# Clustered attention and a rotary token mixer on one core: seven products in batches three and four only, sums of weights made over two plain batches by way of DRAM, a fixed order of all engines from the third batch on

## The chip, the cores and the metric

The kernel runs on one core of one Trainium2 chip. The metric is the device time of one launch in microseconds (us); less is better. The core has five engines that take part: TensorE (PE, matrix products; PEld is its weight load), VectorE (DVE), ScalarE (ACT), GpSimd (POOL) and SyncE (SP), which here issues nearly all DMAs.

## The reference

There are 4 batches, 8 heads, 768 tokens and 64 columns a head, so 512 channels. Queries and keys see each other only if their nearest of 16 centroids is the same; the result x of that attention goes through a mixer of tokens and a product over channels:

```python
mask = q_assign[:, :, :, None] == k_assign[:, :, None, :]
scores = np.where(mask, scale * np.matmul(q, k.transpose(0, 1, 3, 2)), -1000000.0)
...
x = attn_out.transpose(0, 2, 1, 3).reshape(B, S, H * D)    # 4 x 768 x 512

theta = x @ w_theta                                        # 512 x 512
zr, zi = x * np.cos(theta), x * np.sin(theta)
yr = np.einsum('ts,bsd->btd', w_tok_r, zr)                 # 768 x 768
yi = np.einsum('ts,bsd->btd', w_tok_i, zi)
u = x + yr + yi
return u + np.maximum(u @ w_ch, 0.0)                       # 512 x 512
```

## The kernel before

**Two halves.** The attention (lines up to 840) is a loop over units of heads and token tiles and ends at about 450 us. It writes x, with channels on the partitions, into a DRAM buffer for each batch (xT_d). The mixer reads it back. Nothing of the attention is changed.

**The mixer of one batch** works on six tiles of 128 tokens. For each tile *theta* (L927) loads the columns (load_columns, tile xs) and, in another layout, the blocks (load_blocks, L640 to 650, four DMAs, tile xb), and then goes through: a hi part xh on ACT and a lo part xl on DVE (rotation_parts); twelve matmuls with w_theta on PE (rotation_angle, tile tp); reduction of the angle modulo two pi on DVE (rotation_reduce, L666 to 668, tiles kk and rab); abs on ACT (L670); the transpose of xb into xn on DVE (L652); and in *rotate* two sines on ACT (L950) and two products on DVE (L952). Rotations are written two tiles ahead of the mix that uses them (AHEAD = 2).

All matrix products are done with each fp32 operand cut into a hi and a lo part and three products, hi by hi, hi by lo and lo by hi. The hi part is a copy on ACT to PE's own 32-bit type, the lo part a subtraction on POOL or DVE.

**The first batch is mixed plainly** (L985): per tile 48 matmuls into the six PSUM banks of y. The weights wr and wi of all six tiles lie in SBUF as hi and lo. Then *channel_first* (L1138) adds y to x, splits the sum u (add_y), makes u @ w_ch in eight groups of twelve matmuls (channel_products, L1127) and writes out (channel_out, L1134, tile ot and its store L1136).

**Batches two to four use seven products.** Per token tile the two matrices wr and wi and the two halves of zr and zi make a 2 x 2 by 2 x 2 product, for which seven products of sums take the place of eight (ORDER, W_SUM, Z_AT, Y_AT). It works on 256 channels at a time, so each batch has two halves, h = 0 with tiles 0 to 5 and h = 1 with tiles 5 to 0; a half tile has 21 matmuls (mix_forms, L1079). The second half's z go through DRAM: zd is stored by rotate and read back as zb by *split_z* (L1042), which makes the sums of z on DVE (L1054, 1055, 1057) and splits them on ACT and POOL (L1063, 1064). *add_products* (L1083) adds the products to x in seven instructions on DVE (L1088).

**The sums of weights** ("forms", seven 384 KB tiles for each token tile) are made by *make_forms* (L1018) while the first batch runs: it loads wr and wi as fp32 (tile raw), makes a sum on DVE, a copy on ACT and a subtraction on POOL or DVE. The forms of tiles 1, 2 and 3 stay in SBUF in the place of plain weights that are done with. Those of tiles 4, 5 and 0 do not fit; they go to DRAM (w_f) and are loaded again in each batch (*load_forms*, L1038): tile 4's into the four buffers us that later hold u, tiles 5's and 0's into the same seven buffers one after the other (the spares ws0 to ws3 and the first of wr0 and wi0).

**What sets the order.** In the mixer before, each engine's order is decided by the scheduler of the tile framework, from the order in which the code is written and from what is ready by its own reckoning. In the attention, a function *in_order* chains each engine's instructions in the order of the code. SP takes its DMAs in its own row; one that waits holds all behind it.

Of the kernel before, what the change touches and what calls it, by code (L numbers as in the profile page):

```python
# [41 lines left out]
def kernel(  # L42
# [884 lines left out]
    def theta(b, t):  # L927
        n, name = b * NT + t, f"{b}_{t}"
        load_columns(n + 1)
        xs = columns.pop(n) if b else xts[b][:, :, t * P:(t + 1) * P]  # L930
        xh, xl, xn, kk, rab = rotation_tiles(n, name)

        late = n == AHEAD
        rotation_parts(xs, xh, xl, last_out[0] if late else None)
        tp = pm[0].tile([P, 512], F32, tag="bank", name=f"tp{name}") if b else mbank(f"tp{name}")
        with behind(last_rows[0] if late else last_mix[0] if n == AHEAD + 1 else None):
            rotation_angle(xh, xl, tp)
        rotation_reduce(n, tp, kk, rab)
        rotation_turn(n, xn)
        rotate(b, t, rab, xn)  # L940

    z_d = {}

    def rotate(b, t, rab, xn):
        if b == 0:
            z = mz.tile([P, 2, 2, DM], F32R, tag="z", name=f"z{b}_{t}")
        for x, (sc_, bi_) in enumerate(((-1.0, halfpi), (1.0, 0.0))):
            tr = rab[:, x]
            with tc.issue_after(before_sin[0].ins):
                sine = nc.scalar.activation(out=tr, in_=tr, func=AF.Sin, scale=sc_, bias=bi_)  # L950
            with tc.issue_after(before_mul[0].ins):
                nc.vector.tensor_tensor(out=tr, in0=tr, in1=xn, op=ALU.mult)  # L952
            if b == 0:
# [4 lines left out]
        if b:  # L958
            zs[b, t] = rab
            z_d[b, t] = dram.tile([P, 2, DM // 2], F32, tag=f"z{t}", name=f"zd{b}_{t}", bufs=2)  # L960
            nc.sync.dma_start(out=z_d[b, t], in_=rab[:, :, DM // 2:DM])
            return
# [22 lines left out]
    def mix(t):  # L985
        for d in range(NCT):
            for w, (zh, zl) in zip((w_r[t], w_i[t]), zs[0, t]):
# [22 lines left out]
    KEPT = (4, 5, 0)  # L1010
    w_f = {t: dram.tile([P, 7, S], F32, name=f"wf{t}") for t in KEPT}
    PLACE = {
        4: (24, 25, 26, 27, 0, 1, 2), 5: (3, 4, 5, 6, 7, 8, 9), 0: (24, 25, 26, 27, 0, 1, 2),
        1: (10, 11, 12, 13, 14, 15, 3), 2: (4, 5, 6, 7, 8, 9, 16), 3: (17, 18, 19, 20, 21, 22, 23)}
# [3 lines left out]
    def make_forms(t):  # L1018

        raw = u_tile(f"raw{t}").rearrange("p c s -> p (c s)").bitcast(F32)  # L1020
        for x, k in enumerate("ri"):
            nc.sync.dma_start(out=raw[:, x * S:(x + 1) * S], in_=w_d[t, k])
        part = raw.rearrange("p (x n) -> p x n", x=4)
        sums = u_tile(f"sums{t}").rearrange("p c s -> p (c s)").bitcast(F32).rearrange("p (x n) -> p x n", x=4)
        for x, m in enumerate(ORDER):
            to = subs[PLACE[t][x]]
            hi, lo = to[:, 0:HS], to[:, HS:S]
            p, op, q = W_SUM[m]
            src = part[:, p]
            if op is not None:  # L1030
                src = part[:, 1] if m == 6 else sums[:, {4: 0, 3: 1, 1: 2, 7: 3}[m]]
                nc.vector.tensor_tensor(out=src, in0=part[:, p], in1=part[:, q], op=op)
            nc.scalar.copy(out=hi, in_=src)
            (nc.vector if x in (1, 4) else nc.gpsimd).tensor_tensor(out=lo, in0=src, in1=f(hi), op=ALU.subtract)
            if t in KEPT:
                nc.sync.dma_start(out=w_f[t][:, m - 1], in_=f(to))

# [3 lines left out]

    def split_z(b, t, h):  # L1042

        if h == 0:
            src = zs.pop((b, t))
        else:
            src = mzb.tile([P, 2, HD], F32, tag="zb", name=f"zb{b}_{t}")
            nc.sync.dma_start(out=src, in_=z_d.pop((b, t)))
# [34 lines left out]
    def add_products(b, h):  # L1083
# [9 lines left out]
        add(x[:, 0:3:2], twice(4), ALU.add)  # L1093
        add(x[:, 1:4:2], twice(3), ALU.subtract)
        add(x[:, 0:4:3], twice(1), ALU.add)
        add(x[:, 0:4:3], y[:, 2:4, 0:HS], ALU.subtract)
        add(x[:, 1:3], y[:, 2:4, 0:HS], ALU.add)
        add(x[:, 0], product(7), ALU.subtract) if h else add(x[:, 3], product(6), ALU.add)
        add(x[:, 3], product(6), ALU.add) if h else add(x[:, 0], product(7), ALU.subtract)
# [38 lines left out]
    def channel_first():  # L1138
        us = [add_y(0, ch * HS, (ch + 1) * HS) for ch in range(2)]
        for x in range(2 * NCT):  # L1140
            ch, e = divmod(x, NCT)
            cp = (mbank(f"cp0_{x}") if x < 2 else y[:, x - 2])[:, 0:HS]
            channel_products(cp, e, us[ch], range(NCT))
            channel_out(0, e, ch, cp)

    def channel(b, us):
        for x in range(2 * NCT):
            ch, e = divmod(x, NCT)
            cp = product(ORDER[x % 7])
            for ds in ((0, 1), (2, 3)):  # L1150
                channel_products(cp, e, us[2 * ch:2 * ch + 2], ds)
            channel_out(b, e, ch, cp)
# [3 lines left out]
    late_weights = late()  # L1156
    made = {0: (4,), 2: (5, 0), 3: (1,), 4: (2,)}
    for t in range(NT):
        theta(*divmod(t + AHEAD, NT))
        weights_after[0] = splits[min(t + 1, len(splits) - 1)]  # L1160
        next(late_weights, None)
        mix(t)
        for x in made.get(t, ()):
            make_forms(x)
    channel_first()
    load_x(1)
    make_forms(3)
# [3 lines left out]
    four[0] = pm[1].tile([P, 512], F32, tag="bank", name="four")  # L1171

    for b in range(1, B):
        load_forms(4)
        z = split_z(b, 0, 0)
        for t in range(NT):
            if t + AHEAD < NT:
                theta(b, t + AHEAD)
            now, z = z, split_z(b, t + 1, 0) if t + 1 < NT else None
            mix_forms([(t, now)], t == 0, t == NT - 1)  # L1180
            if t == 0:
                load_forms(5)
        if b + 1 < B:
            theta(b + 1, 0)
        z = split_z(b, 5, 1)
        add_products(b, 0)
        for t in (5, 4, 3, 2):
            now, z = z, split_z(b, t - 1, 1)
            mix_forms([(t, now)], t == 5, False)
            if t == 5:  # L1190
                load_forms(0)
            if t == 4:
                split_u_part(b, 0, us, nc.gpsimd)
            if t == 3 and b + 1 < B:
                theta(b + 1, 1)
        mix_forms([(1, z), (0, split_z(b, 0, 1))], False, True)
        add_products(b, 1)
# [56 lines left out]
```

## Time and profile before

| | us |
|---|---|
| median of 3 runs | 911.46 |
| fastest, slowest | 909.16, 914.56 |
| the profiled execution | 912.74 |
| its span | 910.9 |
| PE busy | 802.0 (88%) |
| PEld busy | 591.3 (65%) |
| DVE busy | 681.5 (75%) |
| POOL busy | 556.2 (61%) |
| ACT busy | 420.4 (46%) |

The mean clock granted to TensorE is 0.938 of full speed. The core moves 127.49 MB, a mean of 140 GB/s.

The profile is that of one execution. A view by windows gives, for each stretch of time, its length, each engine's busy time, the clock, the share of the DMA engines' time and the rate. A row of a group gives the line, the engine and the operation, the tiles that are written and read, how many there are, their busy time in us and the mean of one in ns; behind the bar stands the idle time ahead of them and what ended it. A row of the chain of waits gives the time at which a piece of work begins, its length, and in brackets how long its engine had waited and for what.

### The profile page before, as it was taken

Reading aid. Unit: us, or ns where it says so; the run is one execution under the profiler, and the core shown is the slowest. Engines: PE = TensorE matmul, PEld = TensorE weight load, DVE = VectorE, ACT = ScalarE, POOL = GpSimd, SP = SyncE. Lnnn points to the kernel's source line nnn. Section 1 sums busy time; section 2 is a strip of 40 time slices with the busy share of each in tenths; the row PEclk is TensorE's granted clock in tenths of the full one; section 3 lists DMA queues with packets and bytes.
Section 4 is the critical chain, followed back from the end, with each engine's and each line's share of the span. In section 5 each row is a group of like instructions: output and inputs, shape, how many; then the busy total and the mean of one; then the engine's idle time right before and its main releaser. Section 6 shows DMA issues by size and latency. Waiting matters only on the chain. (4 is left out here: it accounts for less than half of the span.)

```text
span 910.9 us, 14439 instructions
## 1 busy us (share of the span) xinstructions
PE 802.0 (88%) x5280; PEld 591.3 (65%) x5280; DVE 681.5 (75%) x847; ACT 420.4 (46%) x843; POOL 556.2 (61%) x333
## 2 busy tenths in 40 slices
PE   9999999999999999979998666687968978789776
PEld 6666666656665666645587545686867957678676
DVE  7689999999999999958678995748565586725641
ACT  3566666676666766645455452323321332203210
POOL 3678898999999989957577756233430335104510
PEclk9999999999999999989999876799879989899889
DMA  3122334443343444344468852584606846165401
GB/s 123 62 86 53 111 121 132 133 136 129 98 133 125 147 150 137 105 158 133 112 175 250 298 173 67 165 299 133 186 1 186 299 122 162 24 211 228 155 12 69
DMA packets 113697, 127.49 MB, mean 140 GB/s; under 512 B 61970, under 2 KB 82588, under 8 KB 113244
## 3 DMA queue, kind: packets, MB, share of 16 engines
q1 hardware_dynamic: 113628, 126.59, 44.1%
q8 instruction: 41, 0.67, 0.3%
q14 instruction: 28, 0.23, 0.1%
HBM read 95.81 MB, written 30.65 MB: 139 GB/s over the span
## 5 line engine op out<-in xcount | busy, mean ns | idle before, releaser
L485 ACT ACTIVATE at<-sc 128x384 f32<-128x384 f32 x384 | 173.9, 493 | 97.9 <-PE m L409 68.7
L431 DVE TENSOR_REDUCE nm<-m 128x1 f32<-128x768 f32 x192 | 180.3, 947 | 29.9 <-PE m L409 26.6
L1064 POOL TENSOR_TENSOR zf<-zt,zf 128x384 fp32r<-128x384 f32 x36 | 37.6, 1045 | 194.1 <-ACT zf L1063 194.1
L496 POOL TENSOR_TENSOR acc<-at,at 128x768 f32<-128x768 f32 x64 | 126.3, 1974 | 40.1 <-ACT at L485 40.1
L409 PE MATMUL m<-hk,hq 64*128 64x384 f32 x384 | 147.9, 386 | 0.2 <-DVE nm L431 0.2
L557 PE MATMUL av<-at,vt 128*64 128x384 f32 x768 | 145.9, 501 | 0.2 <-ACT xt L572 0.2
L496 POOL TENSOR_TENSOR acc<-acc,at 128x768 f32<-128x768 f32 x64 | 131.9, 2061 | 10.9 <-ACT at L485 8.7
L409 PE MATMUL m<-mk,mq 64*128 64x384 f32 x384 | 128.9, 336 | 0.1
L409 PE MATMUL sc<-hq,hk 64*128 64x384 f32 x384 | 117.8, 394 | 6.8 <-ACT at L485 6.6
L409 PEld LDWEIGHTS sc<-hq,hk 64*128 64x128 f32 x384 | 55.3, 185 | 68.8 <-issue 25.3
L409 PE MATMUL sc<-mq,mk 64*128 64x384 f32 x384 | 97.5, 336 | 0.0
L409 PE MATMUL sc<-lq,hk 64*128 64x384 f32 x384 | 97.3, 336 | 0.0
L409 PE MATMUL sc<-hq,lk 64*128 64x384 f32 x384 | 97.3, 335 | 0.0
L1063 ACT CAST zf<-zt 128x384 fp32r<-128x384 f32 x36 | 18.5, 514 | 149.1 <-DVE zt L1055 63.1
L557 PEld LDWEIGHTS av<-at,vt 128*64 128x64 f32 x768 | 46.7, 136 | 59.0 <-issue 54.1
L409 PEld LDWEIGHTS m<-hk,hq 64*128 64x128 f32 x384 | 70.9, 185 | 2.0 <-DVE nm L431 1.4
L409 PEld LDWEIGHTS m<-mk,mq 64*128 64x128 f32 x384 | 71.5, 186 | 0.8 <-DVE mk L374 0.4
L500 DVE TENSOR_TENSOR acc<-acc,acc 128x768 f32<-128x768 f32 x30 | 63.5, 2118 | 0.0
L659 PE MATMUL tp<-wth_hi,xh 128*128 128x512 f32 x96 | 31.9, 461 | 26.4 <-DVE rab L667 26.3
L409 PEld LDWEIGHTS sc<-mq,mk 64*128 64x128 f32 x384 | 54.8, 186 | 0.0
L409 PEld LDWEIGHTS sc<-lq,hk 64*128 64x128 f32 x384 | 54.7, 187 | 0.0
L409 PEld LDWEIGHTS sc<-hq,lk 64*128 64x128 f32 x384 | 54.6, 186 | 0.0
(244 smaller groups left out, 1867.1 us busy)
## 6 DMA issues: line engine op xcount, KB each, us to landing
ws<-wf SPq DMA_DIRECT2D x24, 384.0 KB
u<-wf SPq DMA_DIRECT2D x21, 384.0 KB
vt<-in_v_dram SPq DMA_DIRECT2D x16, 384.0 KB
rb<-sd SPq DMA_DIRECT2D x32, 192.0 KB
xT_d<-xt SPq DMA_DIRECT2D x16, 384.0 KB
xb<-xT_d SPq DMA_DIRECT2D x96, 64.0 KB
out_dram<-ot SPq DMA_DIRECT2D x32, 192.0 KB
rawq<-in_qT_dram SPq DMA_DIRECT2D x15, 384.0 KB
```

The costliest lines, as they stand in the source:

```text
L409: nc.tensor.matmul(out, lhsT=stat[r, cols], rhs=mov[r, over], start=start, stop=stop)
L431: nc.vector.tensor_reduce(out=s["nm", a][:, j, i // 2:i // 2 + 1], in_=s["m", j][:, :, 0:HS], op=ALU.max, axis=AX.XY, negate=True)
L485: last_exp[0] = nc.scalar.activation(out=s["at", a, i][:, j], in_=s["sc", j], func=AF.Exp, scale=SCALE)
L496: last_acc[0] = nc.gpsimd.tensor_tensor(out=s["acc", a, x], in0=prev, in1=at, op=ALU.add)
L500: nc.vector.tensor_tensor(out=s["acc", a, 0], in0=s["acc", a, 0], in1=s["acc", a, 1], op=ALU.add)
L557: nc.tensor.matmul(s["av"][64 * j:64 * j + 64], lhsT=s["vt"][:, i, j, :], rhs=s["at", a, i][:, j], start=(i == 0), stop=(i == NT - 1))
L659: nc.tensor.matmul(tp, lhsT=xx[:, c, :], rhs=w_th[c][k], start=(n == 0), stop=(n == 3 * NCT - 1))
L1063: nc.scalar.copy(out=h_, in_=of)
L1064: nc.gpsimd.tensor_tensor(out=l_, in0=of, in1=f(h_), op=ALU.subtract)
```

## The change

**Two plain batches.** PLAIN = 2: batches one and two are mixed plainly (*mix* and *channel_plain* now take the batch), and only batches three and four use seven products. The plain weights so stay in SBUF until the end of the second batch.

**The forms.** make_forms becomes a generator. Five of its 48 steps are run behind each of ten plain mixes (the second of batch one to the fifth of batch two); a step is the load of one tile's weights or the making of one form. All 42 forms now go through two buffers (ws2 and ws3) to DRAM; the raw weights lie in ws0 and ws1, the sums in two buffers of the pool that later holds zb. All lo parts are made on POOL. Near the end of batch two load_forms brings tiles 0 to 3 back from DRAM, into the places of plain weights.

**The late batches** are written anew, by hand: theta is cut into its parts, of which each has its place in the loop; xl goes from DVE to POOL; reads of zb are issued ahead of the split that uses them (load_z); add_products is cut in two; the first half of u is split on DVE instead of POOL; in channel five groups do their first two blocks of channels before any does the last two; x and tile 4's forms of the next batch are issued behind the channel product. *in_order(begin)* then fixes this order on all five engines.

```diff
+    def theta_parts(n, eng, after=None):
...
+        turning[n] = xh, xl, xn, kk, rab = rotation_tiles(n, f"{b}_{t}")
+        nc.scalar.copy(out=xh, in_=xs)
+            eng.tensor_tensor(out=xl, in0=xs, in1=f(xh), op=ALU.subtract)
...
+    def theta_turn(n):
+        xh, xl, xn, kk, rab, tp = turning[n]
         rotation_reduce(n, tp, kk, rab)
         rotation_turn(n, xn)
...
+    def make_forms():
+        for t in range(NT):
+            for x, k in enumerate("ri"):
+                nc.sync.dma_start(out=f(spares[x]), in_=w_d[t, k])
+            part = [f(spares[x])[:, c:c + HS] for x in range(2) for c in (0, HS)]
+            yield
+            for x, m in enumerate(ORDER):
+                to = spares[2 + (7 * t + x) % 2]
...
+                if op is not None:
+                    src = mzb.tile([P, 2, HD], F32, tag="zb", name=f"sum{t}_{m}").rearrange("p x n -> p (x n)")[:, 0:HS]
+                    nc.vector.tensor_tensor(out=src, in0=part[p], in1=part[q], op=op)
+                nc.scalar.copy(out=hi, in_=src)
+                nc.gpsimd.tensor_tensor(out=lo, in0=src, in1=f(hi), op=ALU.subtract)
                 nc.sync.dma_start(out=w_f[t][:, m - 1], in_=f(to))
+                yield
...
     def channel(b, us):
+        EARLY_GROUPS = 5
...
+        for x in range(EARLY_GROUPS):
+            part(x, (0, 1))
         for x in range(2 * NCT):
+            if x >= EARLY_GROUPS:
+                part(x, (0, 1))
+            part(x, (2, 3))
...
+    for n in range(PLAIN * NT):
+        b, t = divmod(n, NT)
+        theta(*divmod(n + AHEAD, NT))
...
+        mix(b, t)
+        if 0 < n < PLAIN * NT - 1:
+            for _ in range(5):
+                next(new_forms, None)
+        if n == PLAIN * NT - 2:
+            run(new_forms)
+            load_forms(0)
+            load_forms(1)
+        if t == NT - 1:
+            if b == PLAIN - 1:
+                load_forms(2)
+                load_forms(3)
+            channel_plain(b)
+            load_x(b + 1)
...
+    load_forms(4)
+    before(PLAIN * NT + 2)
+    z = split_z(PLAIN, 0, 0)
+    for b in range(PLAIN, B):
+        for t in range(NT - 1):
+            n = b * NT + t
+            done(n + 1)
+            angle(n + 2)
+            before(n + 3)
+            now, z = z, split_z(b, t + 1, 0)
+            mix_forms([(t, now)], t == 0, False)
             if t == 0:
                 load_forms(5)
+            turn(n + 2)
+            if t == NT - 2:
+                load_z(b, 5)
...
+        done(n + 1)
+        now, z = z, split_z(b, 5, 1)
+        load_z(b, 3)
+        mix_forms([(5, now)], False, True)
+        angle(n + 2)
+        add_products(b, 0, 0)
+        now, z = z, split_z(b, 4, 1)
+        load_z(b, 2)
+        add_products(b, 0, 1)
+        before(n + 3)
+        for t in (5, 4, 3, 2, 1, 0):
+            mix_forms([(t, now)], t == 5, t == 0)
...
+                split_u_part(b, 0, us, nc.vector)
+        for k in range(2):
+            add_products(b, 1, k)
+        split_u_part(b, 1, us, nc.vector)
+        if b + 1 < B:
+            z = split_z(b + 1, 0, 0)
+        channel(b, us)
+        if b + 1 < B:
+            load_x(b + 1)
+            load_forms(4)
+    in_order(begin)
```

Here before(n) is theta_parts on POOL, angle(n) theta_angle, turn(n) theta_turn and the two sines, and done(n) the two products on DVE and the store of zd. Rotations are numbered through, n = 6 b + t, so 15 is tile 3 of the third batch.

**Where it moves instructions.** First SP's row, from the last output of the second batch (ot1_1_3) on: xT2 is x of the third batch, xs its columns and xb its blocks (the number behind them is the rotation's), wf5 are tile 5's forms in DRAM. Before:

```order
L1136 DMA out_0_dram<-ot1_1_3_7832 128x384 [waits DMAHW2_49,DVE_49]
L885 DMA xT2_7835<-xT_d2_62 128x3072 [waits DMAHW3_49]
L1040 DMA ws1_6080<-wf5_6120 128x768 [waits DMAHW4_49,PE_49]
...
L1040 DMA ws0_6079<-wf5_6120 128x768 [waits DMAHW2_49,PE_49]
L961 DMA zd2_4_8032<-rab2_4_7998 256x1x256 [waits DMAHW3_49,DVE_49]
L647 DMA xb19_8210<-xT_d3_63 32x16x32 [waits DMAHW4_49,DVE_49]
```

And now:

```order
L1171 DMA out_0_dram<-ot1_1_3_7822 128x384 [waits DMAHW2_49,DVE_49]
L885 DMA xT2_7825<-xT_d2_62 128x3072 [waits DMAHW3_49]
L925 DMA xs15_7839<-xT_d2_62 128x4x128 [waits DMAHW4_49]
L925 DMA xs16_7870<-xT_d2_62 128x4x128 [waits DMAHW5_49]
L1069 DMA ws0_6079<-wf5_6124 128x768 [waits DMAHW6_49]
...
L1069 DMA wi0_hi_115<-wf5_6124 128x768 [waits DMAHW4_49,PE_49]
L647 DMA xb15_7921<-xT_d2_62 32x16x32 [waits DMAHW5_49]
```

Before, the first blocks behind the loads of x and of seven forms are those of rotation 19, in the batch after; now they are those of rotation 15, of which three come ahead of the sixth mix of the batch itself, and the columns of rotations 15 and 16 stand between x and the forms.

Next DVE's row in the same place, one step of the loop over the first half: products of rotation 14 (rab2_2), sums of its z, reduction of the angle of rotation 15 (tp15), and the transpose of its blocks. Before, where the same products stand in the channel product of batch two:

```order
L952 TENSOR_TENSOR rab2_2_7855<-rab2_2_7855,xn2_2_7858 128x512 [waits Activation_49]
L666 TENSOR_SCALAR kk2_3_7934<-tp2_3_7937 128x512 [waits DVE_49,PE_49]
L634 TENSOR_TENSOR xl2_5_8068<-xs17_7996,xh2_5_8067 128x512 [waits DMAHW5_49]
L952 TENSOR_TENSOR rab2_2_7855<-rab2_2_7855,xn2_2_7858 128x512 [waits Activation_49]
L667 SCALAR_TENSOR_TENSOR rab2_3_7930<-kk2_3_7934,tp2_3_7937 128x512 [waits DMAHW5_49,DVE_49,Pool_49]
L1054 TENSOR_TENSOR zt2_2_0_7967<-rab2_2_7855 128x256 [waits DVE_49]
L1055 TENSOR_TENSOR zt2_2_0_7967<-rab2_2_7855 128x128
L652 STREAM_TRANSPOSE xn2_4_8001<-xb16_7955 128x512 [waits DMAHW3_49,DMAHW4_49,DMAHW2_49,DMAHW1_49]
L1134 SCALAR_TENSOR_TENSOR ot1_0_0_7727<-four_7071,xT1_7042 128x384 [waits PE_49]
```

And now, behind the last output of batch two:

```order
L971 TENSOR_TENSOR rab2_2_7841<-rab2_2_7841,xn2_2_7844 128x512 [waits Activation_49] x2
L1087 TENSOR_TENSOR zt2_2_0_7955<-rab2_2_7841 128x256 [waits DVE_49,Pool_49]
L1088 TENSOR_TENSOR zt2_2_0_7955<-rab2_2_7841 128x128
L1090 TENSOR_TENSOR rab2_2_7841<-rab2_2_7841 128x2x128 [waits DVE_49]
L666 TENSOR_SCALAR kk2_3_7876<-tp15_7932 128x512 [waits PE_49]
L667 SCALAR_TENSOR_TENSOR rab2_3_7872<-kk2_3_7876,tp15_7932 128x512 [waits DVE_49,Pool_49]
L668 SCALAR_TENSOR_TENSOR rab2_3_7872<-kk2_3_7876,rab2_3_7872 128x512 [waits DVE_49]
L652 STREAM_TRANSPOSE xn2_3_7875<-xb15_7921 128x512 [waits DMAHW6_49,DMAHW7_49,DMAHW5_49,DMAHW0_49]
L971 TENSOR_TENSOR rab2_3_7872<-rab2_3_7872,xn2_3_7875 128x512 [waits DVE_49,Activation_49]
```

Before, the work of rotations 14 to 17 is woven into the channel product of batch two; now DVE goes through one rotation at a time behind that product, and the transpose of xb15 stands ahead of the products of rotation 15.

Last SP's row in the channel product of the first batch, now: wf2 and wf3 are the stores of forms of tiles 2 and 3, wd4 the raw weights of tile 4, ot0 the outputs.

```order
L1171 DMA out_0_dram<-ot0_0_3_6953 128x384 [waits DMAHW7_49,DVE_49]
L1064 DMA wf3_6122<-ws2_6081 128x768 [waits DMAHW0_49,Pool_49]
L1064 DMA wf3_6122<-ws3_6116 128x768 [waits DMAHW1_49,Pool_49]
...
L1171 DMA out_0_dram<-ot0_1_0_6968 128x384 [waits DMAHW6_49,DVE_49]
L1064 DMA wf3_6122<-ws2_6081 128x768 [waits DMAHW7_49,Pool_49]
L1051 DMA ws1_6080<-wd4i_130 128x768 [waits DMAHW0_49]
L1064 DMA wf3_6122<-ws3_6116 128x768 [waits DMAHW1_49,Pool_49]
L1051 DMA ws0_6079<-wd4r_129 128x768 [waits DMAHW2_49]
...
L1171 DMA out_0_dram<-ot0_1_1_6983 128x384 [waits DMAHW4_49,DVE_49]
```

Before, no store of a form stood among these outputs, as the forms that go to DRAM were done by then; now the outputs and the stores of forms take turns, and each store waits for POOL.

More of the change, by code (lines that the diff above doesn't have):

```diff
@@ L925, in load_columns @@
                 nc.sync.dma_start(out=columns[n], in_=xT_d[b][:, :, t * P:(t + 1) * P])
-    def theta(b, t):
-        n, name = b * NT + t, f"{b}_{t}"
+    PLAIN = 2
+    turning = {}
+    def theta_parts(n, eng, after=None):
+        b, t = divmod(n, NT)
         load_columns(n + 1)
         xs = columns.pop(n) if b else xts[b][:, :, t * P:(t + 1) * P]
[L931 to L936, printed above, removed]
+        turning[n] = xh, xl, xn, kk, rab = rotation_tiles(n, f"{b}_{t}")
+        nc.scalar.copy(out=xh, in_=xs)
+        with behind(after):
+            eng.tensor_tensor(out=xl, in0=xs, in1=f(xh), op=ALU.subtract)
@@ L937, in theta, with theta_angle @@
+    def theta_angle(n, after=None):
+        xh, xl = turning[n][:2]
+        tp = pm[0].tile([P, 512], F32, tag="bank", name=f"tp{n}") if n >= PLAIN * NT else mbank(f"tp{n}")
+        with behind(after):
             rotation_angle(xh, xl, tp)
+        turning[n] += (tp,)
+    def theta_turn(n):
+        xh, xl, xn, kk, rab, tp = turning[n]
         rotation_reduce(n, tp, kk, rab)
         rotation_turn(n, xn)
+    def theta(b, t):
+        n = b * NT + t
+        late = n == AHEAD
+        theta_parts(n, nc.vector, last_out[0] if late else None)
+        theta_angle(n, last_rows[0] if late else last_mix[0] if n == AHEAD + 1 else None)
+        theta_turn(n)
+        xh, xl, xn, kk, rab, tp = turning.pop(n)
@@ L957, in rotate @@
                     nc.gpsimd.tensor_tensor(out=zl, in0=tr, in1=f(zh), op=ALU.subtract)
[L958 to L962, printed above, removed]
+        if b >= PLAIN:
+            return keep_turned(b, t, rab)
         splits.append(split)
@@ L1009 @@
     subs = [x for t in range(NT) for x in (*w_r[t], *w_i[t])] + spares
[L1010 to L1014, printed above, removed]
+    w_f = {t: dram.tile([P, 7, S], F32, name=f"wf{t}") for t in range(NT)}
+    PLACE = {0: (24, 25, 26, 27, 0, 1, 2), 1: range(3, 10), 2: range(10, 17), 3: range(17, 24)}
@@ L1015 @@
     forms = {t: {m: subs[x] for m, x in zip(ORDER, PLACE[t])} for t in range(4)}
     forms[5] = forms[0]
[L1018 to L1035, printed above, removed]
+    def make_forms():
[6 more added lines that the diff above has]
+                to = spares[2 + (7 * t + x) % 2]
+                hi, lo = to[:, 0:HS], to[:, HS:S]
+                p, op, q = W_SUM[m]
+                src = part[p]
+                if op is not None:
[3 more added lines that the diff above has]
+                nc.gpsimd.tensor_tensor(out=lo, in0=src, in1=f(hi), op=ALU.subtract)
@@ L1152, in channel @@
-            channel_out(b, e, ch, cp)
+            channel_out(b, e, ch, product(ORDER[x % 7]))
     rotate(0, 0, first["rab"], first["xn"])
     theta(0, 1)
[L1156 to L1166, printed above, removed]
@@ L1167 @@
-    make_forms(3)
+    late_weights, new_forms = late(), make_forms()
+    for n in range(PLAIN * NT):
+        b, t = divmod(n, NT)
+        theta(*divmod(n + AHEAD, NT))
+        if b == 0:
+            weights_after[0] = splits[n + 1]
+            next(late_weights, None)
+        mix(b, t)
[12 more added lines that the diff above has]
+            load_x(b + 1)
@@ L1171, with before @@
     four[0] = pm[1].tile([P, 512], F32, tag="bank", name="four")
[L1173 to L1180, printed above, removed]
+    begin = len(nc.cur_bb.bb.instructions)
+    last = B * NT
+    def before(n):
+        if n < last:
+            theta_parts(n, nc.gpsimd)
@@ new lines, in angle, with turn, done @@
+    def angle(n):
+        if n < last:
+            theta_angle(n)
+    def turn(n):
+        if n < last:
+            theta_turn(n)
+            sines(turning[n][4])
+    def done(n):
+        if n in turning:
+            turned(n)
+    load_forms(4)
[3 more added lines that the diff above has]
+        for t in range(NT - 1):
+            n = b * NT + t
+            done(n + 1)
[3 more added lines that the diff above has]
+            mix_forms([(t, now)], t == 0, False)
@@ L1181 @@
             if t == 0:
                 load_forms(5)
[L1183 to L1189, printed above, removed]
+            turn(n + 2)
+            if t == NT - 2:
+                load_z(b, 5)
+        n = b * NT + NT - 1
+        load_z(b, 4)
+        done(n + 1)
+        now, z = z, split_z(b, 5, 1)
+        load_z(b, 3)
```

77 lines of the change are left out of this document (48 added, 29 removed).

## The prediction

> **What bounds the kernel now.** I read the windows by stage first, cut where TensorE passes from one stage to the next: the attention part, the first batch's mix, its channel product, then the three batches done with seven products.
>
> ```profile
> 0.00:450.60 450.60, 441.29 (x3588) 272.72 (x3588) 391.48 (x427) 281.19 (x595) 378.36 (x196) 0.99 0.37 118
> 450.60:536.60 86.00, 73.82 (x364) 61.64 (x360) 73.07 (x91) 41.86 (x75) 57.08 (x38) 0.92 0.75 234
> 536.60:598.90 62.30, 35.01 (x138) 30.51 (x138) 42.13 (x68) 20.00 (x41) 29.48 (x26) 0.73 0.46 129
> 598.90:707.90 109.00, 89.00 (x415) 79.49 (x415) 67.05 (x103) 30.11 (x52) 32.00 (x26) 0.89 0.52 160
> 707.90:815.90 108.00, 88.64 (x421) 78.66 (x421) 66.14 (x102) 29.68 (x51) 32.40 (x26) 0.92 0.50 155
> 815.90:910.90 95.00, 74.21 (x360) 68.31 (x360) 41.60 (x61) 17.52 (x30) 26.89 (x22) 0.91 0.36 128
> ```
>
> Columns: stretch, length, busy time of PE, PEld, DVE, ACT and POOL, granted clock, DMA share, GB/s. Attention is full and is not touched; everything happens in the 460.3 us behind 450.6. There PE is neither idle nor full. What full speed is, I take from stretches without a gap:
>
> ```profile
> 465.50:474.20 8.70, 8.57 (x48) 7.26 (x48) 1.00 0.84 225
> 721.70:729.20 7.50, 7.47 (x42) 7.15 (x41) 1.00 0.52 131
> 718.90:721.90 3.00, 2.92 (x12) 2.12 (x12) 1.00 1.00 391
> 695.20:697.70 2.50, 2.38 (x12) 2.06 (x12) 1.00 0.59 144
> ```
>
> These are one token tile of the plain mix (8.57), two half tiles of seven products (7.47, so 3.74 each), one rotation angle (2.92) and one of a batch's eight channel groups (2.38). A plain batch is 6 x 8.57 + 6 x 2.92 + 8 x 2.38 = 88.0 us of PE, one of seven products 44.8 + 17.5 + 19.0 = 81.3. The batches now take 86 + 62.3, 109, 108 and 95. So order and waits bound this half, and PE's own waits in the first batch say which:
>
> ```profile
> 523.02 2.05 PE L659 MATMUL tp<-wth_hi,xh 128*128 128x512 f32 x4 [7.29 <-DVE rab L667]
> 545.60 1.01 PE L1127 MATMUL cp<-uh,wch_hi 128*128 128x384 f32 x2 [9.02 <-ACT uh L1119]
> 557.89 0.69 PE L1127 MATMUL cp<-uh,wch_hi 128*128 128x384 f32 x1 [8.10 <-ACT wch_hi L163]
> 583.31 1.65 PE L1127 MATMUL y<-uh,wch_hi 128*128 128x384 f32 x4 [7.31 <-DVE ot L1134]
> ```
>
> Each is an engine that makes weight sums (make_forms) while PE needs it.
>
> **Batch one, mix: 78 us (now 86).** The old make_forms is L1032 and L1034; their DVE time in this stretch is the fourth number.
>
> ```profile
> 450.60:536.60 86.00, 14.39 (x19) 0.92 0.75 234
> 450.60:536.60 86.00, 8.94 (x7) 20.24 (x16) 0.92 0.75 234
> L1032 DVE TENSOR_TENSOR sums<-raw 128x384 f32<-128x384 f32 x24 | 18.7, 841 | 0.8 <-DMA raw<-wd3i 0.8
> ```
>
> DVE loses 23.3 us and, by the new order, gets 14 sums of 0.84: 73.07 - 23.3 + 11.8 = 61.5. Packed as densely as now (73.07 in 86, 85%) that is 72 us; PE's floor is 6 x (8.57 + 2.92) = 69. But the sums now form a chain: each goes sum, ACT copy, POOL subtraction, store, and the third must wait until the store of the first has left one of two buffers.
>
> ```profile
> L1063 ACT CAST zf<-zt 128x384 fp32r<-128x384 f32 x36 | 18.5, 514 | 149.1 <-DVE zt L1055 63.1 <-PE y L1079 43.4 <-PE four L1079 42.6
> L1034 POOL TENSOR_TENSOR wr_lo<-sums,wr_lo 128x384 fp32r<-128x384 f32 x3 | 3.9, 1311 | 0.1
> 699.03 5.09 DMA out_dram<-ot
> 731.18 2.67 DMA zb<-zd
> ```
>
> A cast of this shape is 0.51 and the subtraction 1.31. A 384 KB store is nowhere alone in the chain of waits; the nearest are 2.67 us (256 KB, quiet) and 5.09 (192 KB, in a queue). With 0.4 to issue, two forms cost 4.9 to 7.3, one 2.4 to 3.7; engines that serve others in between can only add. I take 3.5. Seventeen forms and two reloads of about 4.5 stand ahead of the batch's end, starting at about 460: 9.4 + 17 x 3.5 + 9 = 78. The cover here is DVE's and PE's 72 and 69: up to 3.1 us per form the chain is hidden.
>
> The Trainium skill, "DMA: Bandwidth & Descriptors", section "Anatomy of one DMA", gives 2.0 us plus the bytes at 436 GB/s for a DMA. The quiet 2.67 agrees (2.6 by the rule), the 5.09 does not (2.5). By the rule, as an estimate, a form would cost 2.6 and both stretches would be bound by DVE and PE, some 16 us less together than I reckon.
>
> **Batch one, channel: 46.5 us (now 62.3).** PE's part is 8 x 2.38 + 4 x 2.92 = 31 and some 5 to start. The order puts the output of its second last group behind the stores of four left and seven new forms on SP, and the mix of batch two behind the last output: 11 x 3.5 + 8 for issue and landing of the outputs = 46.5; 36 if the chain is quick, 62 at 5 us per form. The 8.10 us wait for w_ch goes, since that conversion now ends ahead of the batch.
>
> **Batch two, plain: 88 us (now 109).** 6 x 8.57 + 3 x 2.92 + 8 x 2.38 = 79.2, about 5 from the last mix to the first channel group, and six groups that wait 0.65 for the output of the one before (rows below): 88. Its splits (12 casts and 12 subtractions) lie beside mixes of 8.57. It drops 12 split_z and seven-product sums on DVE. Bounds 82 and 100.
>
> **Third and fourth batch, first half.** All engines follow program order. One step on DVE: two products, three ops of split_z, kk and two reductions; then ACT's abs and first sine before the next product can start (the transpose lies beside them).
>
> ```profile
> L952 DVE TENSOR_TENSOR rab<-rab,xn 128x512 f32<-128x512 f32 x28 | 19.0, 709 | 12.3 <-ACT rab L950 12.3
> L1054 DVE TENSOR_TENSOR zt<-rab 128x256 f32<-128x256 f32 x15 | 12.4, 824 | 20.2 <-POOL zf L1064 19.5
> L1055 DVE TENSOR_TENSOR zt<-rab 128x128 f32<-128x128 f32 x15 | 4.2, 282 | 0.0
> L1057 DVE TENSOR_TENSOR rab<-rab 128x256 f32<-128x256 f32 x15 | 6.2, 410 | 0.0
> L666 DVE TENSOR_SCALAR kk<-tp 128x512 int32<-128x512 f32 x13 | 8.9, 681 | 1.3 <-PE tp L659 1.1
> L667 DVE SCALAR_TENSOR_TENSOR rab<-kk,tp 128x512 f32<-128x512 int32 x14 | 9.5, 677 | 0.1
> L668 DVE SCALAR_TENSOR_TENSOR rab<-kk,rab 128x512 f32<-128x512 int32 x14 | 16.1, 1152 | 0.2
> L670 ACT ACTIVATE rab<-rab 128x512 f32<-128x512 f32 x14 | 8.8, 630 | 17.3 <-POOL zf L1064 11.2 <-issue 5.6 <-DVE rab L668 0.5
> L950 ACT ACTIVATE rab<-rab 128x512 f32<-128x512 f32 x14 | 8.6, 616 | 0.0
> ```
>
> 2 x 0.709 + 1.52 + 2.51 + 0.63 + 0.62 + 0.3 for the hops = 7.0 us, against PE's 2.92 + 3.74 = 6.66. So a step is 7.0, bound by this loop. Ahead of it stands a burst: load_x, load_forms and the blocks of the next rotation, in this order on SP, whose rate the full stretch shows.
>
> ```profile
> 708.70:724.40 15.70, 15.70 (x88) 15.19 (x88) 8.68 (x14) 5.50 (x10) 7.02 (x6) 1.00 0.95 365
> u<-wf SPq DMA_DIRECT2D x21, 384.0 KB
> xT<-xT_d SPq DMA_DIRECT2D x3, 1536.0 KB
> ```
>
> 365 GB/s. Now the same burst harms little: the rotations run ahead and SP loads blocks first. After it, xb15 stands behind some 6.5 MB: 17.8 + 2 = 20 us after the batch's start, and its transpose holds DVE until then. From there one product pair and split (2.9), two steps (14) and the POOL end of a split (3) lead to the sixth mix at 40 (35 + 1 without the burst). In the fourth batch xb21 stands behind 7.8 MB, as load_forms(4) joins it: 24.4 us, the sixth mix at 45.
>
> **The rest of these batches.**
>
> ```profile
> L1054 DVE TENSOR_TENSOR zt<-zb 128x256 f32<-128x256 f32 x18 | 16.2, 899 | 32.6 <-DMA zb<-zd 17.3 <-POOL zf L1064 15.3
> L1055 DVE TENSOR_TENSOR zt<-zb 128x128 f32<-128x128 f32 x18 | 10.0, 553 | 0.0
> L1057 DVE TENSOR_TENSOR zb<-zb 128x256 f32<-128x256 f32 x18 | 14.8, 820 | 0.0
> L1088 DVE TENSOR_TENSOR xT<-xT,y 128x768 f32<-128x768 f32 x24 | 22.2, 947 | 19.0 <-PE y L1079 18.8
> 748.42 5.09 PE tp L659 x12
> 884.14 1.01 PE L1127 MATMUL y<-u,wch_hi 128*128 128x384 f32 x2 [3.77 <-DVE xT L1088]
> 895.34 0.62 PE L1127 MATMUL y<-u,wch_hi 128*128 128x384 f32 x2 [0.65 <-DVE ot L1134]
> ```
>
> PE waits at 884.14 for the last addition from y, so y is treated as one tile. The second half's y can be written once DVE has done a split (2.27, after tile 5 was stored and read back, about 6 us into the sixth mix), three additions (2.84), another split and the rest (1.9 and about 1.1): 16.5. Six half mixes are 22.4, a cold start adds 2.2 (5.09 against 2.92), and the channel is 4.9 for additions, 4.8 for four early groups and 16.3 for the rest with its 0.65 waits = 26. Together 67; in the last batch 4 less before (no angle, tile 5 earlier) and 3 for the last store: 66. Now the last batch takes 69 from its sixth mix (837.8) to the end, which is the upper bound. Third batch: 40 + 67 = 107 (now 108); fourth: 45 + 66 = 111 (now 95, with one rotation where it now gets four).
>
> The Trainium skill, "TensorE: Matmul & The Clock Gate", section "Why this matters for your kernels", warns of idle gaps above some 3 us, behind which the array runs at half rate; it speaks against this order, which leaves two or three such gaps in each late batch. The 5.09 above, behind a wait of 3.4 us, agrees, and that price is in the sum.
>
> **Sum.** 450.6 + 78 + 46.5 + 88 + 107 + 111 = 881 us of span. The profiled execution took 912.74 for a span of 910.9, 0.14% above the median of 911.46. Adding the same 1.8: **882 us**.
>
> **Rivals.** *The burst and the chain are hidden* (DVE-bound 72 + 1 and 36.5 in batch one, 4 and 9 less at the two starts): 882 - 5 - 10 - 13 = 854. For it: SP has eight transfers in flight and nothing says that blocks cannot pass; against: DMA is at 0.95 in the burst. Chance 0.22. *The chain of forms binds*: above 3.5 us, each us per form costs 17 + 11 = 28 us. From 4.75 it is slower than now by over 0.5%; at 5 it is 924. For it: four in-order queues per form, DMA at 0.75 in batch one; against: 3.7 is the upper end of the rows. Chance 0.12. *The plain batch gains nothing*: if batch two waits as batch one does now (148 where PE needs 88, so 124 with the four rotations already done), 882 + 36 = 918, and with a chain of 3.1 it is 907, within 0.5%. Chance 0.08. *POOL slows DVE*, since xl goes to POOL: with products of 1.11 instead of 0.71, eight steps cost 7 us more, which stays in my range. My forecast, 865 to 896, has 0.52, other outcomes 0.06.
>
> The range of 848 to 914 reaches from the first rival's lower side past the third, and leaves out most of the chain that binds. Half a per cent is about what a measurement of this kernel can tell from no change. Faster by more: 0.52 + 0.22 + 0.04 = 0.78; within: 0.09; slower: 0.13.
>
> **What would show it.** First mix of batch two at about 575 (before 570: chain hidden; after 595: it binds, with ACT casts of make_forms waiting for stores). Batch two 88 long with PE's clock near 1. After its end a wait of PE for xh of tile 15 and of DVE for xb15, about 20 us in; for xb21 some 24 us into the last batch. Steps of 7.0 on DVE. A wait of some 10 us of PE between the halves. If the late batches take under 95 each, the reading of the burst is wrong; if batch two takes over 100, that of the plain batch.

## The result and the profile after

The changed kernel takes **886.82 us**, the median of 3 runs (885.21 to 889.29), against 911.46 before; the ratio is 0.973, with a 95% interval of 0.967 to 0.979. It is faster, 4.8 us above the forecast of 882 and within its range. The profiled execution has a span of 883.4 us where 881 was reckoned.

The windows by stage of the kernel after, with the columns of the prediction's first fence: first batch's mix, its channel product, second batch, third, fourth. The attention ahead of them takes 450.2 us.

```profile
450.20:521.70 71.50, 69.11 (x364) 57.41 (x360) 57.48 (x71) 32.79 (x57) 48.21 (x32) 1.00 0.69 201
521.70:576.00 54.30, 31.46 (x144) 27.35 (x144) 36.58 (x59) 24.35 (x46) 33.67 (x30) 0.84 0.71 229
576.00:660.40 84.40, 78.30 (x424) 67.60 (x424) 37.90 (x59) 23.77 (x44) 37.12 (x33) 1.00 0.82 278
660.40:772.90 112.50, 85.81 (x406) 77.47 (x407) 62.15 (x90) 30.09 (x53) 37.92 (x31) 0.88 0.48 146
772.90:883.40 110.50, 82.30 (x397) 74.83 (x395) 52.12 (x84) 22.96 (x40) 27.27 (x24) 0.90 0.43 141
```

| stage | before | forecast | after |
|---|---|---|---|
| first batch, mix | 86.0 | 78 | 71.5 |
| first batch, channel | 62.3 | 46.5 | 54.3 |
| second batch | 109 | 88 | 84.4 |
| third batch | 108 | 107 | 112.5 |
| fourth batch | 95 | 111 | 110.5 |

The first two batches give 47 us, and the last two take 20 of them back. TensorE's share of a stage shows where: 78.3 of 84.4 us in the plain second batch at full clock, 85.8 of 112.5 and 82.3 of 110.5 at a clock of 0.88 to 0.90 in the late ones.

What waits, first in the channel product of the first batch (waits of PE from 515 to 576 us; columns: us in total, number, longest):

```profile
PE cp L1162 <- ACT uh L1154: 17.7, 2, 17.4
PE y L1162 <- DVE ot L1169: 2.4, 3, 1.0
```

One wait of 17.4 us stands between the last mix and the first channel product. The stores of forms up to that point, as one line of the program:

```profile
L1064 SPq DMA_DIRECT2D wf<-ws x17: 319/382/657, 465.1 to 537.8; - x17
```

Seventeen forms have been stored when u begins, from 465.1 to 537.8: 72.7 us in 16 intervals, 4.5 us each, reloads of the raw weights among them.

Then the start of the third batch. First the waits of PE for the hi part of columns, from 640 us to the end:

```profile
PE tp L659 <- ACT xh L935: 12.0, 2, 8.6
```

Two pieces of work there, on ACT and on DVE (start, length, instruction, and in brackets the idle time before it and what ended it):

```profile
671.77 0.62 ACT L935 CAST xh<-xs 128x512 fp32r<-128x512 f32 x1 [34.38 <-DMA xs<-xT_d]
674.55 2.39 DVE L971 TENSOR_TENSOR rab<-rab,xn 128x512 f32<-128x512 f32 x2 [14.20 <-ACT rab L964]
```

And SP's own row there (start, length, and what is issued):

```profile
661.18 0.42 SPq L885 DMA_DIRECT2D xT<-xT_d  x1
661.66 1.97 SPq L925 DMA_DIRECT2D xs<-xT_d  x2
663.67 5.24 SPq L1069 DMA_DIRECT2D ws<-wf  x4
...
672.55 3.93 SPq L647 DMA_DIRECT2D xb<-xT_d  x4
```

The columns of rotation 15 (xs) are issued behind the 1.5 MB of x, and its blocks (xb) behind seven forms (four of them in the third row), 12 us into the batch. PE waits 8.6 us for the hi part of those columns. DVE's 14.2 us go back to the same columns: the products at 674.55 are those of rotation 14, and its sines stand in ACT's row behind the hi part of rotation 15, for whose columns ACT sat idle until 671.77. For the blocks nothing waits in this batch; their transpose at 682.05 (shown under e4) has no idle time ahead of it. In the fourth batch the blocks hold DVE, those of rotation 21, until 24.8 us after the batch's start:

```profile
797.66 0.71 DVE L652 STREAM_TRANSPOSE xn<-xb 128x512 f32<-128x512 f32 x1 [13.21 <-DMA xb<-xT_d]
```

### The profile page after: what moved, and what is told of

The parts are those of the page before. It is cut to its first block, busy times and chain, and to the rows that moved or that the text cites. A ratio compares the mean times of both kernels' runs of the same rounds, so it can differ in the third digit from the quotient of the medians.

```text
span 883.4 us, 14497 instructions
## 1 busy us (share of the span) xinstructions
PE 788.0 (89%) x5316; PEld 576.5 (65%) x5316; DVE 640.4 (72%) x789; ACT 415.3 (47%) x835; POOL 563.6 (64%) x345
## 5 line engine op out<-in xcount | busy, mean ns | idle before, releaser
L1097 POOL TENSOR_TENSOR zf<-zt,zf 128x384 fp32r<-128x384 f32 x24 | 24.8, 1031 | 82.1 <-ACT zf L1096 82.1
L1063 POOL TENSOR_TENSOR ws<-sum,ws 128x384 fp32r<-128x384 f32 x30 | 35.2, 1178 | 33.2 <-ACT ws L1062 33.2
L1024 PE MATMUL y<-wr_hi,z 128*128 128x512 f32 (+1 forms) x192 | 49.9, 341 | 4.1 <-DVE ot L1169 2.5
```

The source lines that it names most:

```text
L1024: last_mix[0] = nc.tensor.matmul(y_at(d, c0, c1), lhsT=zz[:, d * P:(d + 1) * P], rhs=ww[:, c0:c1], start=first and lead, stop=last, skip_g ...
L1063: nc.gpsimd.tensor_tensor(out=lo, in0=src, in1=f(hi), op=ALU.subtract)
L1097: nc.gpsimd.tensor_tensor(out=l_, in0=of, in1=f(h_), op=ALU.subtract)
```

## The experiments

Every kernel was timed against the kernel before on the same chip. The changed kernel's ratio to it is 0.973.

| run | median us | ratio, 95% interval |
|---|---|---|
| e1 late batches as before | 871.36 | 0.9575 (0.9546 to 0.9603) |
| e2 free order | 860.87 | 0.9456 (0.9425 to 0.9486) |
| e3 burst later | 870.95 | 0.9553 (0.9524 to 0.9582) |
| e4 xl on DVE | 882.85 | 0.9694 (0.9665 to 0.9723) |
| e5 all four batches plain | 824.45 | 0.9058 (0.9031 to 0.9084) |
| e6 steps 4 and 6 | 886.86 | 0.9747 (0.9729 to 0.9765) |
| e7 no stores of forms | 888.82 | 0.9771 (0.9752 to 0.9789) |
| e8 no forms made | 861.55 | 0.9465 (0.9443 to 0.9486) |
| e9 forms held | 883.15 | 0.9690 (0.9668 to 0.9712) |
| e10 SP's row free | 868.74 | 0.9535 (0.9499 to 0.9572) |
| e11 free order, burst later | 859.59 | 0.9418 (0.9387 to 0.9449) |
| e12 only SP's row fixed | 886.19 | 0.9728 (0.9708 to 0.9749) |

### The late batches: who holds them

**e1, the late batches as in the kernel before.** The loop of before for batches three and four, with plain first and second batches.

```diff
+    for b in range(PLAIN, B):
+        load_forms(4)
+        z = split_z(b, 0, 0)
+        for t in range(NT):
+            if t + AHEAD < NT:
+                theta(b, t + AHEAD)
...
-    in_order(begin)
```

> Two plain batches and the forms by way of DRAM stay; batches three and four are written as in the kernel before, with no fixed order. Theory of the prediction (the late batches are held by one rotation after the other, 7 us each, whoever orders them): third and fourth together take what they took before, 108 + 95, and the three to four rotations that no longer run ahead, about 7 us each, so 224 to 231 against 223 now: 885 to 895 us. Rival 1, the fixed order holds the rotations back, and a free order would run them in the channel products: 865 to 875. Rival 2, the fixed order is what brings the gain: over 900.

Measured 871.36, within the first rival's band. Its third and fourth batch, in the windows of that run:

```profile
667.08:775.85 108.77, 89.95 (x414) 79.79 (x414) 65.71 (x101) 29.66 (x51) 32.48 (x26) 0.89 0.48 150
775.85:869.00 93.15, 73.42 (x360) 67.62 (x360) 41.72 (x61) 17.52 (x30) 26.91 (x22) 0.92 0.35 131
```

They take 109 and 93 as in the kernel before (108 and 95), behind a second batch that ends 6.7 us later and has the angles of three rotations of the third in its channel product instead of one. So the two plain batches and their forms are worth some 40 us (911 to 871), and the late batches' new form, text and fixed order together, gives some 15 of them back (871 to 887). The rest of the 20 us in the table by stage is work that moved from the second batch into the third.

**e2, free order.** The new text of the late batches, with the scheduler's order.

```diff
-    in_order(begin)
```

> The changed kernel without in_order(begin), the new text of the late batches otherwise as it is. Theory of the prediction (what holds a step is the loop from DVE to ACT and back, which no order shortens): 882 to 892 us, third and fourth batch each within 4 us of 112 and 110. Rival, the free order weaves the rotations of the next batch into the channel products as in the kernel before: 870 or less. Second rival, the scheduler puts loads or splits ahead that wait and holds an engine: over 895.

Measured 860.87: 26 us faster than with the fixed order, and the theory of the prediction fell. Windows of its third and fourth batch:

```profile
666.25:767.00 100.75, 83.53 (x414) 76.58 (x414) 63.98 (x97) 29.52 (x51) 37.06 (x29) 0.95 0.53 161
767.00:857.10 90.10, 71.53 (x360) 66.28 (x360) 40.55 (x64) 17.45 (x30) 24.04 (x20) 0.92 0.38 137
```

And SP's row ahead of that third batch:

```profile
650.00 0.58 SPq L925 DMA_DIRECT2D xs<-xT_d  x1
...
653.41 2.47 SPq L647 DMA_DIRECT2D xb<-xT_d  x3
...
661.97 2.62 SPq L647 DMA_DIRECT2D xb<-xT_d  x4
...
667.24 0.65 SPq L885 DMA_DIRECT2D xT<-xT_d  x1
667.98 1.76 SPq L1069 DMA_DIRECT2D ws<-wf  x3
```

Columns and blocks now stand among the outputs of the second batch, up to 17 us ahead of x and of the forms. The text is better than the one of before (e1, 871); the fixed order hid it.

**e3, the burst later.** The order stays fixed on all engines, but x and the forms of tiles 4 and 5 are issued behind the blocks of the first rotations.

```diff
-            if t == 0:
-                load_forms(5)
             turn(n + 2)
+            if t < 2:
+                load_forms(4 + t)
+            if t == 2:
+                load_x(b)
...
-            load_x(b + 1)
-            load_forms(4)
```

> In the late batches x and the forms of tiles 4 and 5 are loaded behind the blocks of the first rotations instead of ahead of them. Theory of the prediction (columns and blocks of rotation 15, and of 21, stand behind the burst): PE's wait of 8.6 us for xh of rotation 15 and DVE's of 14.2 us for its sines go, likewise some 9 us at the start of the fourth batch: 14 us less, 870 to 875 us. Rival, the burst is only in the way of something that waits anyway (the loop of DVE and ACT, or the forms and x are then late for the mixes of tiles 4 and 5 and for the additions): 884 to 890.

Measured 870.95, as the theory had it. PE's waits for xh from 640 to 700 us, a stretch that ends 37 us into its third batch:

```profile
PE tp L659 <- ACT xh L935: 2.4, 1, 2.4
```

The wait of 8.6 us for xh is down to 2.4. DVE's longest wait for sines from 640 to 740 us is 1.2 us instead of 14.2, though one of 6.2 us for an angle has come.

**e10, e12 and e11: which engine's row.** The last in_order(begin) fixes all but SP (e10) or SP alone (e12); e11 joins e2 and e3.

```diff
+    ENGINES = ENGINES[:-1]    # e12: ENGINES[-1:]
     in_order(begin)
```

> in_order(begin) fixes PE, DVE, ACT and POOL, and SP's row is left to the scheduler. Theory (of the 26 us that the fixed order costs, 16 are SP's row, in which the blocks stand behind x and the forms, as the run with the late burst showed; the rest is that PE and DVE do no rotations in the channel products): 868 to 874 us. Rival (SP's row follows what the other engines' fixed rows free, so nothing moves): 883 to 889.

> in_order(begin) fixes SP's row alone, and PE, DVE, ACT and POOL are left to the scheduler. Theory (SP's row is 16 of the 26 us, as it keeps the columns of rotation 15 behind x, and so no rotation can go ahead of the burst whatever the others' order): 873 to 882 us. Rival (the order of PE and DVE is what counts, SP's row is much the same either way): 858 to 866.

> The late loads of x and forms together with the free order of all engines. Theory (in the free order columns and blocks of the next rotations are loaded ahead of the burst already, so both edits take away the same wait): 857 to 864 us, as with the free order alone. Rival (they add): 843 to 850.

Measured 868.74, 886.19 and 859.59. With SP's row fixed, 886 to 887 us come out whether the other four engines are fixed or not (e12, after); with SP free, 869 and 861. So SP's row alone costs 25 us where the others are free, more than the 16 expected, and 18 where they are fixed; the other four rows cost 8, and only once SP's is free. In e10 PE waits nowhere for xh in the start of its third batch (655 to 700 us); its longest wait there is the first row below. In e12, with SP's row fixed, the waits for xh are back (second row, 640 us to the end):

```profile
PE y L1162 <- DVE ot L1169: 2.3, 2, 1.7
```

```profile
PE tp L659 <- ACT xh L935: 14.1, 4, 5.1
```

e11 equals e2 within their intervals. The late burst and the free order do not add, as they would if they took away different waits.

**e4, xl on DVE.** In the late rotations the lo part of the columns goes back to DVE.

```diff
-            theta_parts(n, nc.gpsimd)
+            theta_parts(n, nc.vector)
```

> Only xl of the late rotations goes back from POOL to DVE. Theory (POOL's subtraction slows the reduction at L668 beside it: 1.79 us in the steps of the third batch, 0.69 where POOL is idle): a step of 7.95 us falls to about 7.5 (1.1 less, 0.68 more), ten steps: 4 to 5 us less, 882 us, and L668 at 0.7. Rival (POOL does not slow it; DVE just has one instruction more in its loop): steps of 8.6, 6 us more, 893 us.

Measured 882.85, the size that was expected, though its interval and that of the changed kernel overlap. The reason was another. First a step on DVE in the changed kernel, from transpose to transpose (start, length, instruction, idle time before):

```profile
682.05 0.70 DVE L652 STREAM_TRANSPOSE xn<-xb 128x512 f32<-128x512 f32 x1
683.55 1.31 DVE L971 TENSOR_TENSOR rab<-rab,xn 128x512 f32<-128x512 f32 x2 [0.80 <-ACT rab L964]
684.96 1.38 DVE L1087 TENSOR_TENSOR zt<-rab 128x256 f32<-128x256 f32 x1
...
686.80 0.68 DVE L666 TENSOR_SCALAR kk<-tp 128x512 int32<-128x512 f32 x1
687.58 0.69 DVE L667 SCALAR_TENSOR_TENSOR rab<-kk,tp 128x512 f32<-128x512 int32 x1
688.30 1.80 DVE L668 SCALAR_TENSOR_TENSOR rab<-kk,rab 128x512 f32<-128x512 int32 x1
690.02 0.70 DVE L652 STREAM_TRANSPOSE xn<-xb 128x512 f32<-128x512 f32 x1
```

And in e4:

```profile
690.39 0.70 DVE L652 STREAM_TRANSPOSE xn<-xb 128x512 f32<-128x512 f32 x1
691.88 1.31 DVE L971 TENSOR_TENSOR rab<-rab,xn 128x512 f32<-128x512 f32 x2 [0.79 <-ACT rab L964]
693.11 0.68 DVE L937 TENSOR_TENSOR xl<-xs,xh 128x512 fp32r<-128x512 f32 x1
693.71 0.42 DVE L1087 TENSOR_TENSOR zt<-rab 128x256 f32<-128x256 f32 x1
...
695.36 0.69 DVE L667 SCALAR_TENSOR_TENSOR rab<-kk,tp 128x512 f32<-128x512 int32 x1
696.08 1.80 DVE L668 SCALAR_TENSOR_TENSOR rab<-kk,rab 128x512 f32<-128x512 int32 x1
697.80 0.70 DVE L652 STREAM_TRANSPOSE xn<-xb 128x512 f32<-128x512 f32 x1
```

A step falls from 7.97 to 7.41 us, and all of it lies between the start of the products and that of L668 (4.75 us, then 4.20). L668 stays at 1.80, as another subtraction on POOL, that of the split (zf), still runs beside it; it is the sum zt (L1087) that goes from 1.38 to 0.42 when xl leaves POOL, and pays for the 0.68 that DVE takes on.

### The forms

**e6, fewer steps in the first batch.** Four steps behind each mix of the first batch, six behind those of the second.

```diff
-            for _ in range(5):
+            for _ in range(4 if b == 0 else 6):
```

> Four steps of the forms behind each plain mix of the first batch and six behind those of the second, in place of five and five. Theory (the chain of forms, about 4.5 us each in the first batch, holds DVE, ACT and POOL ahead of the first channel product, where PE waits 17.4 us): five steps less there take 10 to 14 us off that wait, the second batch has room for them; 873 to 877 us. Rival 1 (the wait is for the rotations and the split of z): no change, 884 to 889. Rival 2 (the forms then end late, and their loads come late for the third batch): 886 or over, with the wait at the first channel product gone and a new one at the third batch.

Measured 886.86, no change; but it tells nothing of the theory. In the rows of the engines 14 sums and 17 copies stand ahead of the first addition of y, in this kernel as in the changed one: the scheduler put the forms in the same places, though the text had changed.

**e7 and e8, no stores and no forms.** In both, loads of forms read plain weights.

```diff
-                nc.sync.dma_start(out=w_f[t][:, m - 1], in_=f(to))
+++ e8: make_forms is empty
```

> The forms are made but not stored, and in the place of each load of a form the plain weights of the same size are read, so the output is not the reference's. Theory (a form costs 4.5 us because the copy on ACT waits until the store of the form two before has left the buffer): a form falls to 2 us or less, the wait of 17.4 us ahead of the first channel product falls to 5 or less, 870 to 875 us. Rival (engines that serve rotations, splits and late weights too hold the chain, not the stores): the wait stays above 12, 880 or over.

> The forms are neither made nor stored, and in the place of each load of a form the plain weights of the same size are read, so the output is not the reference's. It bounds what making them costs. Theory: the wait of 17.4 us falls to about 4, the channel product of the first batch by 2 to 4, the second batch by up to 4: 865 to 870 us. Rival (the late weights and rotations of the first batch hold it): 878 or over.

Measured 888.82 and 861.55. The waits of PE ahead of the first channel product, in e7 and in e8:

```profile
PE cp L1161 <- ACT uh L1153: 15.3, 1, 15.3
```

```profile
PE cp L1147 <- ACT uh L1139: 2.3, 1, 2.3
```

Making the forms costs 25 us, and 15 of the 17.4 us wait are theirs; some 20 of the 25 are there when the second batch begins (at 555.5 us in e8, at 576.0 in the changed kernel). Without the stores the wait hardly falls, but there the scheduler puts 23 forms ahead of the addition of y instead of 17. What a store adds to a form is thus not settled by e7. In the changed kernel the copies wait 7.9 us for stores up to that point (the trace of L1064: "ACT ws L1062: 7.9, 7").

**e9, forms held behind the first addition of y**, so that 8 stand ahead of it.

```diff
+                    with behind(held.get("sum")):
+                        nc.vector.tensor_tensor(out=src, in0=part[p], in1=part[q], op=op)
...
-            for _ in range(5):
+            for _ in range(2 if b == 0 else 8):
```

> Two steps of the forms behind each mix of the first batch and eight behind those of the second, and what is left of the forms is held behind the last addition of y in the first batch on DVE, ACT and POOL, so that 8 forms instead of 17 stand ahead of the first channel product. Theory (each form ahead of it costs DVE, ACT and POOL some 2 us of the 17.4 us wait; without any form it was 2.3): the wait falls to 3 to 8 us, the first batch ends 10 us earlier; 33 forms are left for some 112 us, 3.4 us each, so they just fit or end some 5 us late: 868 to 880 us. Rival (the chain takes what it takes and the wait only moves to the third batch's loads): 884 or over.

Measured 883.15. Its waits of PE, from 500 to 560 us and from 645 to 672:

```profile
PE cp L1167 <- ACT uh L1159: 7.9, 1, 7.9
```

```profile
PE y L1117 <- DMA ws<-wf: 11.9, 1, 11.9
PE four L1117 <- DMA ws<-wf: 4.3, 1, 4.3
```

The wait falls from 17.4 to 7.9, and the third batch begins at 645.5 instead of 660.4. There it waits 16 us for forms that are made, stored and loaded too late, and the third batch takes 123 us. The time is nearer to the rival, and its kind was right: the forms are work for DVE, ACT, POOL and SP, and in both places where they were put, PE waits for them.

### A version without forms

**e5, all four batches plain.** PLAIN = 4; make_forms, the loads of forms and the late loop go.

```diff
-    PLAIN = 2
+    PLAIN = 4
...
-        theta(*divmod(n + AHEAD, NT))
+        if n + AHEAD < B * NT:
+            theta(*divmod(n + AHEAD, NT))
```

> All four batches are mixed plainly; no forms are made, stored or loaded, and nothing of the late batches' text is left. If a plain batch takes what TensorE needs and a few us, as the second one did (84.4): 450 + 113 (the first batch, without the 12 us of its wait for u that I put down to the forms) + 84 + 90 + 87 = 824, 815 to 840 us. Rival, the second batch was quick only because nothing but rotations and forms lay beside it and four rotations had been done before: later plain batches of 100 and more, 850 or over.

Measured **824.45**, a ratio of 0.906 to the kernel before, within the expected 815 to 840: it beats both. The batches behind the first take 92, 93 and 81 us, where 84, 90 and 87 were expected. Its windows (first mix, first channel product, batches two, three and four):

```profile
450.20:518.40 68.20, 67.92 (x364) 57.50 (x360) 53.14 (x68) 31.43 (x52) 35.78 (x23) 1.00 0.49 131
518.40:557.30 38.90, 31.52 (x145) 27.92 (x144) 20.89 (x40) 12.63 (x23) 10.25 (x10) 0.91 0.35 91
557.30:649.40 92.10, 87.04 (x456) 75.45 (x457) 35.63 (x62) 25.31 (x44) 22.96 (x20) 0.98 0.27 69
649.40:742.00 92.60, 87.05 (x456) 75.47 (x457) 34.24 (x60) 24.13 (x42) 22.94 (x20) 0.98 0.21 54
742.00:823.20 81.20, 71.06 (x384) 61.73 (x384) 14.48 (x29) 12.32 (x22) 17.96 (x16) 0.98 0.12 42
```

In the last two batches DVE is busy 34 and 14 us instead of 62 and 52, and PE 94% and 88% of the time. Seven products save 6.7 us of PE in a batch (88.0 against 81.3 in the prediction) and lose more than that in waits even in the best order seen, 100.8 and 90.1 in e2 against 92.6 and 81.2 here, with the making of the forms still to be paid.

## Why the prediction came out right, step by step

- **The total** was 2.4 us of span too low, with errors of -6.5, +7.8, -3.6, +5.5 and -0.5 us in its five terms. So that it came so near is in part luck: errors that cancel.
- **Batch one, mix and channel** (78 + 46.5 = 124.5): 125.8. Seventeen forms stood ahead, as reckoned, and cost 4.5 us each with the reloads, where 3.5 and 9 for two reloads make 4.0. The delay by the forms was right in size and put in the wrong places: into the mix (78, where the case with a hidden chain has 72) and into the outputs on SP's row (46.5, where it has 36.5). The rotations run ahead of the mixes, so PE finishes these undisturbed (71.5). The channel product took 37 us from its first group (539 to 576), and PE's waits for outputs in it are 2.4 us. The queue of forms meets u instead, in the wait of 17.4 us between the two; e8 and e9 show that it is theirs. Of the four waits that the prediction read as the work of make_forms, the one of 8.10 us was for the conversion of w_ch.
- **Batch two** (88): 84.4, with PE at full clock; its first mix began at 576.0, where 575 was named. Right, a little too careful with the gaps.
- **A step of 7.0 us on DVE**: 7.97. By the starts in the step shown under e4, the products take 1.41 (1.42 reckoned), the sums and the difference of the split 1.84 (1.52), the reduction 3.22 (2.51), and ACT's part up to the next products 1.50 (1.55). So two terms were too small. L668 entered with its mean of 1.15; it takes 0.69 alone and 1.80 beside a subtraction on POOL, and in these steps it has one beside it. The zt sum is slowed by xl as well; in a step of the fourth batch without xl, from 804.98 to 811.99, it takes 0.42 and the step 7.01. The rival of a slowed DVE named the products of L971, which take 0.65 each here: its kind was right, and its price, 7 us in eight steps, about the size.
- **The burst**: that columns and blocks stand behind it was read from SP's row and came true. In the fourth batch the mechanism is the forecast one, DVE waiting for xb21 until 24.8 us after the start (24.4 reckoned, though 7.8 MB at 365 GB/s and 2 us make 23.4). In the third the transpose of xb15 begins after 21.7 us (20 reckoned), but not because its blocks are late: the columns are, and they hold PE and ACT. That the times agree there is luck. The sixth mix began 43.2 us into the third batch (40 reckoned; the slower steps are most of the difference) and 43.8 into the fourth (45). The price of the burst in its rival, 4 + 9 us, is near the 16 that e3 takes away. What the prediction lacked is a rival in which SP's row is free: then the rotations run in the channel product of the batch before, and the late batches take 191 us in e2, where its lowest case had 103 + 102. The largest thing that this change gives away, 18 us by the order of one queue and 26 by the fixed order as a whole, it saw by half.
- **Behind the sixth mix** (67 and 66): 69.3 and 66.7. PE's waits for the additions between the halves are 2.6 and 2.9 us in the third batch and 3.5 in the fourth, where some 10 were named. The bound of 69 us taken from the kernel before was misread: from 837.8 to the end of its span at 910.9 are 73.
- **The clock**: angles behind a wait of 0.7 and 1.3 us take 2.97 us each, behind waits of 3.4 and 5.9 us 4.6, behind 8.6 us 5.2. This agrees with the warning of the Trainium skill, "TensorE: Matmul & The Clock Gate", section "Why this matters for your kernels", on gaps above some 3 us. The mean clock of the late batches is 0.88 and 0.90 here, that of the second batch 1.00.

Not tried: a third buffer for the forms, and single parts of the late text such as the five early groups.

## What to carry to other kernels

Fixing an order by hand fixes the DMA queue too, and there a load of 4 MB that is needed in 40 us goes ahead of one of 256 KB that is needed at once: fix the compute engines, and check the queue's row apart. Arithmetic that saves 8% of TensorE's work is worth having only if TensorE is what the stage waits for, and its preparation has to be counted as work for the engines that do the waiting. An edit to the text moves nothing if a scheduler decides the order; look at the rows before reading a "no change" as an answer.

## What was not expected of the hardware

How much a subtraction on POOL beside it costs an operation on DVE. Of the ten L668 from 640 us on in the changed kernel, six begin 0.03 to 0.05 us behind a subtraction on POOL and take 1.77 to 1.81 us; the four with POOL idle take 0.69. The zt sum takes 0.42 or 1.38. POOL's row in e4, to be held against L667 at 695.36 and L668 at 696.08 in the fence above:

```profile
695.07 1.02 POOL L1097 TENSOR_TENSOR zf<-zt,zf 128x384 fp32r<-128x384 f32 x1 [5.15 <-ACT zf L1096]
696.03 1.30 POOL L1097 TENSOR_TENSOR zf<-rab,zf 128x512 fp32r<-128x512 f32 x1
```

The second subtraction begins 0.05 us before L668 and ends at 697.33; L668 ends 0.55 later, a little less than its own 0.69. So DVE was held nearly until POOL was done. The Trainium skill, "SBUF — State Buffer", section "Who interferes with whom", says that a DVE instruction with two SBUF inputs contends with a GpSimd instruction that reads SBUF, over ports that only one of them can hold, and that the order of issue decides which one is held up. That agrees: L668 and L1087 read two tiles in SBUF. L667 is the same operation as L668 on the same shape, but reads the angle in PSUM as its second input; it ran from 695.36 to 696.05 beside the first subtraction and took its 0.69.
